# Windowed attention with a routed expert layer on one core: where the second products of nine expert slots are formed by seven products of halves

## The chip, the core and the metric

One Trainium2 chip, one core of it. The program has one launch. The metric is the device time in microseconds (us), the median of three runs; lower is better. Engines: TensorE (PE, with its weight loads PEld), VectorE (DVE), ScalarE (ACT), GpSimd (POOL), SyncE (SP), which issues most transfers.

## The reference

```python
def reference(q, k, v, modality_id, w_gate, modality_bias, w1, w2):
    # q, k, v: (8, 8, 576, 64), float32: batch, heads, positions, head size
    scores = q @ k.T / sqrt(64)                  # per batch and head
    scores = where(0 <= row - column < 64, scores, -1e9)
    x = softmax(scores) @ v                      # -> x: (4608, 512), the 8 heads side by side
    logits = x @ w_gate + modality_bias[modality_id]        # 8 experts
    e = argmax(logits, axis=1); g = softmax(logits)[e]
    out[i] = g[i] * (relu(x[i] @ w1[e]) @ w2[e])            # w1: 8 x 512 x 1024, w2: 8 x 1024 x 512
```

Each of the 4608 tokens goes to one expert. With these inputs the busiest expert has 2289 tokens and the second 1841.

## The kernel before

**Attention.** The sequence is cut into blocks of 64 positions; a step `s` of the main loop handles a pair of blocks with all heads, 36 pairs, and each pair passes through the loop's parts in successive steps (scores in step s, probabilities turned and multiplied with v, then logits and routing up to five steps later), so the loop has 40 steps. Every second step a group of 256 tokens is routed; its rows are written to `xs_scratch` in memory, sorted by expert, by indirect transfers from POOL's queue (`scatter`).

**Slots.** The expert layer works on slots of 256 tokens of one expert, read back from `xs_scratch` by a transfer from SP (`load_slot`, called by `fetch`). To keep float32 accuracy, every operand is split into a high and a low part (ACT rounds the high part, DVE subtracts to get the low one), and each product is formed as hi·hi + hi·lo + lo·hi on PE. A slot has the first products (hidden layer, `first`: 96 matmuls of 128x256) and the second ones. A *plain* slot forms the second products directly (`second`: 48 matmuls of 128x512). A *fast* slot cuts both matrices in halves and uses seven products of sums and differences of halves where eight are usual (`fast_step`, `product`: 84 matmuls of 128x256); `left_of`, `right_of` and `rest_of` build the token side's sums on DVE and ACT, `fast_out` adds the seven results up on DVE. The weight side's sums (the names `b11`, `t1` to `t4` in `factors`) are formed once per expert: four differences on POOL for each quarter of w2, then casts on ACT and subtractions on DVE (`combine`).

**Order.** `slot_pieces` is a generator that gives out one *piece* of a slot's PE work at a time (16 for a plain slot, 15 for a fast one). Steps 12 to 39 beside attention call it four times each (`gap`); the seven slots that this covers are plain. After the last step a loop takes the remaining pieces one after the other. `later` holds the work of other engines that follows a piece. The expert with the most expected tokens is X (index 0), the second Y (index 1); both are chosen at the start from the gate's bias. Small tables worked out on DVE (`plan`, and further behind attention) find each slot's row in `xs_scratch`; `EARLY` lists after which routed group T a slot of X or Y is planned, `LATE` the slots that are planned when all tokens are known: those of X and Y, and of "any" expert (whatever is left). Unfilled places would point at dummy rows.

**Weights.** A piece of weights is 128x512 (16 per expert). `weights(s)` loads one, and splits those that have come; behind attention, the pieces of the "any" experts follow the list `swaps` with their positions. `Whi0`/`Wlo0` hold X. `Whi1`/`Wlo1` hold Y, and later an "any" expert. In before, beside attention run four slots of X and three of Y; behind it one of Y, five fast ones of X, two of Y kept back (`held`), three of any and a half slot for what remains.

**Pads.** Behind the last row of each expert in `xs_scratch`, `pad_rows` copies a block of filler rows (SP's queue): eight copies behind attention, before the loads of late slots.

## Time and profile before

| | |
|---|---|
| median of 3 runs | 642.9 us (642.09 to 645.06) |
| profiled execution, its own time | 640.05 us |
| its span | 638.3 us |
| granted clock, mean | 0.999 |
| start-up and steps 0 to 11 | 0 to 98 us |
| steps 12 to 39, with the first seven slots | 98 to 366.5 us |
| remaining slots | 366.5 to 627 us |
| tail (last outputs) | 627 to 638.3 us |

The page lists busy time by engine, then the span in forty slices, the transfers, the chain of work that ended last, and the costliest groups of instructions. Rows of groups read: line, engine, operation, output from inputs, shape and count, then busy time. Rows of a timeline read: start and length in us, engine, line, operation, and in brackets how long the engine was idle before it and on what it waited. `L415` is the matmul in `second`, `L290` that in `first`, `L374` that in `product`, `L265` the turn of a slot's tokens, `L119` the subtraction in `split_lo`, `L301` the one that gives `hl`, `L1405` to `L1411` the weight side's sums, `L892` the indirect write of routed rows, `L206` the load of a slot's tokens, `L1264` the pads.

### The profile page before, as it was taken

What the parts mean: (1) busy time and instruction counts of PE and PEld (TensorE: products, weight loads), DVE (VectorE), ACT (ScalarE), POOL (GpSimd) and SP (SyncE); (2) the same over time, 40 slices, a digit from 0 to 9 for tenths busy, and PEclk for the clock granted to TensorE, in tenths of its full rate; (3) what the DMA queues carried; (4) which work ended last, traced back from release to release, by engine and by line L of the source; (5) the groups of instructions that cost most, each with busy time, mean ns of one, the idle gap of its engine ahead of it and who ended that gap; (6) DMA issues with size and microseconds to landing.
All of it is one profiled execution on the core that took longest, in us unless ns stands there. A gap on an engine that the chain in (4) does not pass through costs nothing. (4 is left out here: it accounts for less than half of the span.)

```text
span 638.3 us, 17909 instructions
## 1 busy us (share of the span) xinstructions
PE 611.4 (96%) x6689; PEld 558.0 (87%) x6689; DVE 403.5 (63%) x1571; ACT 328.5 (51%) x1005; POOL 154.3 (24%) x337
## 2 busy tenths in 40 slices
PE   6898888999999999999999999999999999999996
PEld 3787777898989889899898988999999989989886
DVE  2978977666776676756654255876746755666611
ACT  3888876656665656455644123533433444554411
POOL 5324432042032213320322255111011011101102
PEclk9999999999999999999999999999999999999999
DMA  9989894774876674552323476021105076777300
GB/s 170 184 194 249 233 222 133 180 167 121 184 177 151 140 177 106 142 137 57 111 75 110 123 205 242 20 67 51 50 34 198 16 223 198 211 243 240 109 1 36
DMA packets 142120, 90.72 MB, mean 142 GB/s; under 512 B 118954, under 2 KB 118992, under 8 KB 141904
## 3 DMA queue, kind: packets, MB, share of 16 engines
q1 hardware_dynamic: 133344, 70.07, 44.8%
q0 software_dynamic: 5856, 18.92, 8.0%
q10 hardware_dynamic: 2832, 0.59, 0.6%
q8 instruction: 53, 0.87, 0.6%
q14 instruction: 35, 0.29, 0.2%
HBM read 70.11 MB, written 23.91 MB: 147 GB/s over the span
## 5 line engine op out<-in xcount | busy, mean ns | idle before, releaser
L290 PE MATMUL em<-xh,Whi 128*128 128x256 f32 x400 | 102.8, 291 | 1.2 <-DVE xl L196 1.0
L290 PE MATMUL em<-xh,Wlo 128*128 128x256 f32 x400 | 98.2, 279 | 0.0
L765 ACT ACTIVATE ss<-ss,mn 128x128 f32<-128x128 f32 x240 | 94.0, 397 | 2.6 <-DVE mn L753 2.6
L429 POOL DMA_INDIRECT out_dram<-y,id x36 | 37.5, 1042 | 219.3 <-DVE y L394 74.4
L415 PE MATMUL y<-Whi,hh 128*128 128x512 f32 x208 | 86.6, 416 | 0.0
L415 PE MATMUL y<-Wlo,hh 128*128 128x512 f32 x208 | 81.6, 392 | 2.2 <-DVE e_take L154 2.2
L415 PE MATMUL y<-Whi,hl 128*128 128x512 f32 x208 | 81.5, 392 | 0.0
L290 PEld LDWEIGHTS em<-xh,Whi 128*128 128x128 f32 x400 | 75.3, 188 | 2.2 <-DVE xl L196 1.6
L290 PEld LDWEIGHTS em<-xh,Wlo 128*128 128x128 f32 x400 | 75.4, 188 | 0.5
L774 ACT COPY pT<-tp 128x512 f32<-128x512 f32 x59 | 32.6, 589 | 78.6 <-PE tp L595 74.3
L753 DVE CUSTOM_DVE_ANT_0 ss<-sp,masks 128x128 f32<-128x128 f32 x240 | 53.5, 287 | 18.4 <-PE sp L736 16.2
L301 DVE SCALAR_TENSOR_TENSOR hl<-em,hh 128x512 fp32r<-128x512 f32 x40 | 27.6, 690 | 57.1 <-ACT hh L300 57.1
L290 PE MATMUL em<-xl,Whi 128*128 128x256 f32 x400 | 63.2, 280 | 0.0
L892 POOL DMA_INDIRECT xs_scratch<-xa,idx x36 | 36.2, 1007 | 81.4 <-DVE lm L835 26.2
L290 PEld LDWEIGHTS em<-xl,Whi 128*128 128x128 f32 x400 | 53.7, 188 | 0.0
L791 PEld LDWEIGHTS av<-ve,pT 128*64 128x64 f32 x576 | 36.3, 138 | 16.4 <-issue 8.4
L300 ACT ACTIVATE hh<-em 128x512 fp32r<-128x512 f32 x40 | 23.6, 591 | 48.1 <-PE em L290 44.1
L791 PE MATMUL av<-ve,pT 128*64 128x64 f32 x576 | 41.0, 225 | 7.2 <-DVE ve L666 3.3
L415 PEld LDWEIGHTS y<-Whi,hl 128*128 128x128 f32 x208 | 39.0, 188 | 8.8
L765 ACT ACTIVATION_READ_ACCUMULATOR ss<-ss,mn 128x1 f32 x240 | 46.4, 193 | 0.0
L415 PEld LDWEIGHTS y<-Wlo,hh 128*128 128x128 f32 x208 | 39.2, 189 | 7.6 <-DVE e_take L154 2.5
L415 PEld LDWEIGHTS y<-Whi,hh 128*128 128x128 f32 x208 | 39.1, 188 | 5.6 <-ACT Whi L112 0.3
(341 smaller groups left out, 1535.3 us busy)
## 6 DMA issues: line engine op xcount, KB each, us to landing
xt<-xs_scratch SPq DMA_DIRECT2D x18, 514.0 KB
y<-in_moe_w_dram SPq DMA_DIRECT2D x32, 256.0 KB
vo<-in_v_dram SPq DMA_DIRECT2D x27, 256.0 KB
vo<-in_moe_w_dram SPq DMA_DIRECT2D x27, 256.0 KB
ss<-in_moe_w_dram SPq DMA_DIRECT2D x27, 256.0 KB
pT<-in_moe_w_dram SPq DMA_DIRECT2D x18, 256.0 KB
xs_scratch<-xs_scratch SPq DMA_DIRECT2D x8, 514.0 KB
qk<-in_q_dram SPq DMA_DIRECT2D x16, 256.0 KB
```

Of the source, the lines that this page charges most:

```text
L290: nc.tensor.matmul(out=hb[:, i * TP:(i + 1) * TP], lhsT=w[buf][:, c0:c0 + P], rhs=x[:, c * TP:(c + 1) * TP], start=(n == 0), stop=(n == le ...
L300: nc.scalar.activation(out=hh, in_=hb, func=AF.Relu),
L301: nc.vector.scalar_tensor_tensor(out=hl, in0=hb, scalar=0.0, in1=hh.bitcast(F32), op0=ALU.max, op1=ALU.subtract)))
L415: nc.tensor.matmul(out=sl["y", t], lhsT=h[:, i * TP + t * P:i * TP + (t + 1) * P], rhs=w[buf][:, c0:c0 + DM], start=(k == 0 and n == 0), s ...
L429: ins = nc.gpsimd.indirect_dma_start(out=out, out_offset=bass.IndirectOffsetOnAxis(ap=sl["id"][:, t:t + 1], axis=0), in_=y, in_offset=None ...
L753: nc.vector.tensor_tensor_reduce(out=ss[a][:, hp, :], in0=sp[a][:, hp * P:(hp + 1) * P], in1=mask, scale=-1.0 / 8.0, scalar=3.0e38, op0=AL ...
L765: nc.scalar.activation(out=ss[a][:, hp, :], in_=ss[a][:, hp, :], func=AF.Exp, bias=mn[:, h:h + 1], scale=-1.0, accum_out=sm[:, h:h + 1])
L774: nc.scalar.copy(out=pT, in_=pp)
L791: nc.tensor.matmul(out=av[c * W64:(c + 1) * W64, 2 * hp + a], lhsT=pT[:, i:i + W64], rhs=(vo if c else ve)[p][:, 2 * hp + a, :], start=Tru ...
L892: ins = nc.gpsimd.indirect_dma_start(out=xs, out_offset=bass.IndirectOffsetOnAxis(ap=idx[:, j:j + 1], axis=0), in_=xg[j], in_offset=None)
```

## The change

- The seven slots beside attention are all X's, and plain (`PLAIN = 7`). Behind attention come two slots of X and seven of Y, all nine fast, then two of any expert and the half slot. `EARLY` has one slot each for T = 2, 4, ..., 16; the doubled plans and `held` go.
- Memory for weights is cut into X's four tiles `M0` to `M3` and the stock `S0`, `S1`, `S2`. X's sums for fast slots lie in `S0`; Y's w1 in `S1`, `S2`. Y's w2 comes late, into `M0`, `M1`, which held X's w1, when the last X slot no longer needs it. The first "any" expert goes to `M2`, `M3` and `S0` during four of Y's slots, one weight piece per four products.
- X's sums are formed in steps 16 to 19 beside attention, Y's in steps 36 to 39 (`SUMS`, `sums_load`, `combine`, `sums_parts`), with one more call of `weights(s)` in step 13; then Y's w1 from step 20 on. Y's w2 itself and the one factor left out follow behind attention (`y_quarters`, `y_fourth`), with three of the four POOL differences made a second time.
- In a fast slot, the next slot's tokens are fetched three products later, and the token side's sums are formed after the first and second product (`sums_of`, `run_after`), the rest after the third and fourth.
- Ten pad copies (X's and Y's first, then the eight experts', those already done sent to spare rows), from a later point on, one each four products.

```diff
-    EARLY = ((2, (0, 1)), (4, (0, 1)), (6, (0, 1)), (8, (0, 1)), (9, (1, 2)), (10, (1, 2)), (11, (1, 2)),
-             (12, (0, 2)), (13, (0, 2)), (15, (0, 2)))
+    EARLY = tuple((T, (0, 1)) for T in (2, 4, 6, 8, 10, 12, 14, 16))
-    LATE = ((0, False), (0, False), (0, True), (1, True), (0, True), (1, True))
-    NPIN = 2
+    LATE = ((0, False),) + ((1, False),) * 7 + ((2, True), (3, True), (2, True))
+    NPIN = 7
-    MIXED = 7
+    PLAIN = 7
...
-    stock = [wpool.tile([P, 2 * WC], F32, name=f"W{part}1") for part in ("hi", "lo")]
-    Whi = [wpool.tile([P, 2 * WC], F32R, name="Whi0"), None]
-    Wlo = [wpool.tile([P, 2 * WC], F32R, name="Wlo0"), None]
+    stock = [wpool.tile([P, 2 * WC], F32, name="S0")] + [wpool.tile([P, WC], F32, name=f"S{n}") for n in (1, 2)]
+    w_x = [wpool.tile([P, WC], F32R, name=f"M{n}") for n in range(4)]
+    store = {0: w_x}
+    def wap(buf, part, c0, n):
+        return store[buf][part + 2 * (c0 // WC)][:, c0 % WC:c0 % WC + n]
...
-        fast = n_slots[0] > MIXED and buf == 0 and whichever is None
+            fast=n_slots[0] > PLAIN and whichever is None)
...
             if i == 1 and sl["fast"]:
                 later.append(lambda: (left_of if k < 2 else right_of)(sl, k % 2, hb))
+                if k >= 2:
+                    after.append(lambda: sums_of(sl, k % 2, hb))
...
             if sl["fast"]:
-                first(sl, 1, 0)
-                yield
-                first(sl, 1, 1)
-                yield
-                first(sl, 2, 0)
-                yield
-                nxt = fetch()
-                first(sl, 2, 1)
-                yield
+                for k in (1, 2):
+                    for i in range(2):
+                        first(sl, k, i)
+                        yield
                 fast_step(sl, "p1")
+                run_after()
                 yield
                 first(sl, 3, 0)
                 yield
+                nxt = fetch()
                 first(sl, 3, 1)
                 yield
                 fast_step(sl, "p7")
-                later.append(lambda: rest_of(sl))
+                run_after()
                 yield
                 fast_step(sl, "p2")
+                run_after()
+                later.append(lambda: rest_of(sl, "s2"))
                 yield
                 fast_step(sl, "p4")
+                later.append(lambda: rest_of(sl, "s4"))
...
-            pieces.extend((x, c) for x in range(2) for c in PIECE_ORDER)
+            pieces.extend((0, c) for c in PIECE_ORDER)
...
+    def combine(x, y, full=True):
+        b11, b12, b21, b22 = x[:, 0:half], x[:, half:DM], y[:, 0:half], y[:, half:DM]
+        for o, a, b in ((b11, b12, b11), (b12, b22, b12), (b22, b22, b11), (b21, b21, b22)):
+            if full or o is not b12:
+                nc.gpsimd.tensor_tensor(out=o, in0=a, in1=b, op=ALU.subtract)
+    def put_parts(src, hi, lo):
+        nc.scalar.copy(out=hi, in_=src)
+        nc.vector.tensor_tensor(out=lo, in0=src, in1=hi.bitcast(F32), op=ALU.subtract)
+    def sums_parts(x, j):
+        a, b = sums_x.pop((x, j))
+        f13, f2 = combos[x][0:2]
+        put_parts(a, f13[0][:, j, :], f13[1][:, j, :])
+        put_parts(b[:, half:DM], f2[0][:, j, :], f2[1][:, j, :])
+        if not x:
+            f4 = combos[x][2]
+            put_parts(b[:, 0:half], f4[0][:, j, :], f4[1][:, j, :])
+    SUMS = {FIRST + 4 + j: (0, j) for j in range(4)}
+    SUMS.update({NPR + j: (1, j) for j in range(4)})
...
     for s in range(NPR + 4):
+        if s == FIRST + 8:
+            store[1] = store[3] = [wpool.tile([P, WC], F32R, name=f"S{n}") for n in (1, 2)] + w_x[0:2]
+            pieces.extend((1, c) for c in (0, 2, 4, 6, 1, 3, 5, 7))
-        n_tick = 6 if s < FIRST else 5
+        n_tick = 6 if s < FIRST or j else 5
...
             high(s)
+        if s in SUMS:
+            combine(*sums_x[SUMS[s]])
...
         if n_gap > 0 and s != FIRST:
+            if s == FIRST + 1:
+                weights(s)
             gap(it, True)
...
             weights(s)
+        if s in SUMS:
+            sums_parts(*SUMS[s])
+        if s + 1 in SUMS:
+            sums_load(*SUMS[s + 1])
...
+    at_ = begin_of[slot_y - 1] + 7
+    pairs_y = [[load(at_, 8 + j + 4 * i, lambda: evs[1]) for i in range(2)] for j in range(4)]
+    for n, i in enumerate((0, 5, 6, 7)):
+        task(at_ + i, y_quarters(n), *pairs_y[n])
+    for n, i in enumerate((8, 10, 13, 14)):
+        task(at_ + i, y_fourth(n), *pairs_y[n])
+    for x, (buf, at_, gap_) in enumerate(((2, begin_of[slot_y + 1], 4), (3, begin_of[slot_a], 1), (2, begin_of[slot_a + 1], 1))):
+        for n, c in enumerate(PIECE_ORDER):
+            task(at_ + n * gap_, whole_piece(buf, c, ("any", x)), load(at_ + n * gap_, c, lambda x=x: any_of(x)))
...
     while next(it, "end") != "end":
...
-        if pads and waited > SLOT_PIECES:
+        if len(pads) > E + 1:
+            if t > begin_of[slot_y - 2]:
+                pad_rows(pads.pop(0))
+        elif len(pads) > E:
+            if not todo or todo[0][2] != 0 or todo[0][1] is not None:
+                pad_rows(pads.pop(0))
+        elif pads and t >= begin_of[slot_y] + 16 and waited % 4 == 0:
             pad_rows(pads.pop(0))
```

The order of instructions on three engines, at the places where other engines wait or are waited for. First DVE in step 14, before: `hl` is the low part of a hidden layer (128x512), `Wlo0` the low part of X's weights, the rows `L836` to `L848` belong to the routing.

```order
L301 SCALAR_TENSOR_TENSOR hl_2285<-em_2223,hh_2284 128x512 [waits Activation_49]
L836 TENSOR_TENSOR lg_1977<-lg_1977,lm_2167 128x16
L840 SCALAR_TENSOR_TENSOR wn_2169<-lg_1977,desc_194 128x16 [waits DVE_49]
L842 TENSOR_REDUCE wm_2170<-wn_2169 128x2 [waits DVE_49]
L843 TENSOR_TENSOR oh_1803<-wn_2169,wm_2170 128x16 [waits DVE_49]
L848 TENSOR_REDUCE oh_2171<-oh_1803 128x8 [waits DVE_49]
L119 TENSOR_TENSOR Wlo0_67<-y_2101,Whi0_66 128x512 [waits DMAHW6_49]
```

After, the same stretch (`M3` is the low part of X's second matrix, `M2` its high part):

```order
L848 TENSOR_TENSOR lg_1980<-lg_1980,lm_2179 128x16 [waits DVE_49]
L117 TENSOR_TENSOR M3_70<-y_2062,M2_69 128x512 [waits DMAHW6_49,Activation_49]
L153 TENSOR_TENSOR e_n_p_2093<-sel2_71,cnt_2091 1x8
L158 TENSOR_REDUCE e_n_2094<-e_n_p_2093 1x1 [waits DVE_49]
L147 SCALAR_TENSOR_TENSOR e_at_2095<-e_n_2094,room2_229,row2_72 1x1 [waits DVE_49]
L141 TENSOR_SCALAR rows_0_4_2096<-e_at_2095 1x1 [waits DVE_49]
L714 COPY kT_101<-tp_2294 128x2x2x128 [waits PE_49]
L304 SCALAR_TENSOR_TENSOR hl_2293<-em_2235,hh_2292 128x512 [waits Activation_49]
```

The piece of weights whose low part stood behind `hl` and the routing's rows now stands ahead of them.

Next POOL around the last routed group, before: `gate` and `id` come from a slot's tokens, `xa` are the rows that are written to `xs_scratch`.

```order
L274 COPY gate_6640<-xt_6529 128x2 [waits DMAHW1_49]
L276 CAST id_6642<-xt_6529 128x2 [waits DMASW3_49,DMASW0_49]
L891 COPY xa4_105<-idc_202 128x1 [waits DMASW7_49]
L892 DMA xs_scratch<-xa4_105,idx_6605 39168x514 [waits DVE_49,Pool_49]
L891 COPY xa0_101<-idc_202 128x1 [waits DMASW1_49]
L892 DMA xs_scratch<-xa0_101,idx_6605 39168x514 [waits Pool_49]
```

After:

```order
L1176 TENSOR_TENSOR vo_6588<-vo_6588 128x256 [waits DMAHW0_49,PE_49]
L1176 TENSOR_TENSOR vo_6588<-ss_6589,vo_6588 128x256 [waits DMAHW1_49,Pool_49]
L1176 TENSOR_TENSOR ss_6589<-ss_6589,vo_6588 128x256 [waits Activation_49,Pool_49]
L1176 TENSOR_TENSOR ss_6589<-ss_6589 128x256 [waits Pool_49]
L903 COPY xa4_108<-idc_205 128x1 [waits DMASW7_49]
L904 DMA xs_scratch<-xa4_108,idx_6642 39680x514 [waits DVE_49,Pool_49]
L903 COPY xa0_104<-idc_205 128x1 [waits DMASW0_49]
L904 DMA xs_scratch<-xa0_104,idx_6642 39680x514 [waits Pool_49]
```

The four differences of Y's last quarter stand ahead of the last two writes of routed rows.

Last SP at the end of attention, before: `vo` and `ss` take pieces of w2 for the sums, `masks` is the room for tables.

```order
L204 TENSOR_LOAD rows_2_12_5154
L206 DMA xt_6803<-xs_scratch 128x2x514 [waits DMAHW0_49,DMAHW1_49,PE_49,Pool_49]
L105 DMA vo_6860<-in_moe_w2_dram 128x512
L105 DMA ss_6862<-in_moe_w2_dram 128x512 [waits DMAHW2_49]
L1263 TENSOR_LOAD masks_143 [waits DVE_49,Pool_49]
L1264 DMA xs_scratch<-xs_scratch 16x8224 [waits DMAHW3_49,DMAHW0_49]
```

After:

```order
L201 TENSOR_LOAD rows_0_16_6463 [waits DVE_49]
L203 DMA xt_6551<-xs_scratch 128x2x514 [waits DMASW5_49,DMASW4_49,DMAHW7_49,DMASW1_49,DMASW0_49]
L108 DMA vo_6588<-in_moe_w2_dram 128x512 [waits DMAHW0_49,PE_49]
L108 DMA ss_6589<-in_moe_w2_dram 128x512 [waits DMAHW2_49,DVE_49,Pool_49]
L1357 TENSOR_LOAD masks_146 [waits DVE_49,Pool_49]
L1358 DMA xs_scratch<-xs_scratch 16x8224 [waits DMAHW7_49]
L201 TENSOR_LOAD masks_146 [waits DVE_49,Pool_49]
L203 DMA xt_6892<-xs_scratch 128x2x514 [waits DMASW7_49,DMAHW2_49,DMASW6_49,DMAHW3_49,PE_49,Pool_49]
```

The load of slot 7's tokens now stands ahead of the last loads for the sums, and waits for the writes of the group that planned it; the first pad copy stands ahead of the next slot's load.

More of the change, by code (lines that the diff above doesn't have):

```diff
@@ L198, in ready @@
     def ready(sl, c0):
-        c = c0 // WCH
-        assert (sl["buf"], c) not in pieces + [r[1:] for r in raws + halves]
-        assert sl["any"] is None or (sl["any"], c) not in [w[2:] for w in swaps]
+        assert (sl["key"], c0 // WCH) in have
     def load_slot(row_ap, late, nb):
@@ L219, in tile_window_attn_moe @@
     later = []
+    after = []
+    mixed = []
     scattered = []
     n_slots = [0]
-    n_early = [0]
-    held = []
     factors = {}
@@ L234, in bank, with run_after @@
         return ps_t.tile([P, 512], F32, name="tp")
+    def run_after():
+        later.extend(after)
+        after.clear()
     def run_later():
@@ L243, in fetch @@
         row, late, buf, whichever, need = todo.pop(0)
-        assert late is not None or not pads
+        assert late is not None or len(pads) <= {0: E + 1, 1: E}.get(buf, 0)
         assert late is None or late in scattered
@@ L248, in fetch @@
         n_slots[0] += 1
-        fast = n_slots[0] > MIXED and buf == 0 and whichever is None
-        return dict(xt=load_slot(row, late, nb), buf=buf, any=whichever, nb=nb, fast=fast)
+        return dict(
+            xt=load_slot(row, late, nb), buf=buf, nb=nb, key=buf if whichever is None else ("any", whichever),
+            fast=n_slots[0] > PLAIN and whichever is None)
     def slot_pieces():
@@ L285, in first @@
             hi, lo = sl["x"]
-            mm = [(w, c, hi) for c in range(NC1) for w in (Whi, Wlo)] + [(Whi, c, lo) for c in range(NC1)]
+            mm = [(w, c, hi) for c in range(NC1) for w in (0, 1)] + [(0, c, lo) for c in range(NC1)]
             for n, (w, c, x) in enumerate(mm):
@@ L410, in second @@
             hi, lo = sl["h", k]
-            mm = [(h, w, i) for i in range(2) for h, w in ((hi, Whi), (hi, Wlo), (lo, Whi))]
+            mm = [(h, w, i) for i in range(2) for h, w in ((hi, 0), (hi, 1), (lo, 0))]
             for n, (h, w, i) in enumerate(mm):
@@ L439, in half_first @@
             hi, lo = sl["x"]
-            mm = [(x, w, c) for c in range(NC1) for x, w in ((hi, Whi), (hi, Wlo), (lo, Whi))]
+            mm = [(x, w, c) for c in range(NC1) for x, w in ((hi, 0), (hi, 1), (lo, 0))]
             for m, (x, w, c) in enumerate(mm):
@@ L464, in half_second @@
             yp = ps_m.tile([P, DM], F32, name=f"y{a}")
[L465 removed]
+            mm = [(w, n, c, lo) for n in range(2) for c in range(HP) for w, lo in ((0, 0), (1, 0), (0, 1))]
             for m, (w, n, c, lo) in enumerate(mm):
@@ L939, in plan @@
         stt(pl, nm, take, float(TP), room, ALU.mult, ALU.add, out=room)
-        for i, x in reversed(list(enumerate(range(xs_.start, xs_.stop)))):
-            (held if x and n_early[0] > MIXED else todo).append((rows[0:1, i:i + 1], f"scatter_after_{T}", x, None, need))
-            n_early[0] += 1
+        for i, x in enumerate(range(xs_.start, xs_.stop)):
+            todo.append((rows[0:1, i:i + 1], f"scatter_after_{T}", x, None, need))
     def choose():
@@ L1366, in tile_window_attn_moe @@
             n_of[buf] += 1
-            continue
-        last_use[buf] = len(early) + n_any - 1
     last.append(True)
-    ahead = []
+    tick(ready_p - issued[0], table=True)
     waited = 0
-    t13 = [att.tile([P, 2, HP, GBLK, W64], F32R, name=nm).rearrange("p g h j i -> p (g h j i)") for nm in ("kT", "qT")]
-    t2 = [work.tile([P, 2, H, D], F32R, name="qk", bufs=2).rearrange("p t h d -> p (t h d)") for _ in range(2)]
-    half = DM // 2
-    inner = [x[0][:, WC:2 * WC].rearrange("p (c n) -> p c n", n=DM) for x in (Whi, Wlo)]
@@ new lines, in tile_window_attn_moe, with load, task @@
+    slot_y = len(EARLY) + 1
+    slot_a = slot_y + 7
+    w2 = [x.rearrange("p (c n) -> p c n", n=DM) for x in w_x[0:2]]
+    make_factors(1, *combos[1], w2, half)
+    store[2] = [w_x[2], w_x[3], sums_home[:, 0:WC], sums_home[:, WC:2 * WC]]
+    loads = []
+    tasks = []
+    raw_of = {}
+    def load(pos, c, ev):
+        loads.append([pos, c, ev, None])
+        return len(loads) - 1
+    def task(pos, f, *ids):
+        for i in ids:
+            loads[i][3] = len(tasks)
+        tasks.append((pos, f, ids))
@@ L1440, in tile_window_attn_moe @@
+        while n_load < len(loads) and loads[n_load][0] <= t + RAWS and (
+                n_load < RAWS or loads[n_load - RAWS][3] < n_task):
+            _, c, ev, _ = loads[n_load]
+            raw_of[n_load] = load_piece(raw_tile(), ev(), c)
+            n_load += 1
+        if n_task < len(tasks) and tasks[n_task][0] <= t:
+            _, f, ids = tasks[n_task]
+            f(*(raw_of[i] for i in ids))
+            n_task += 1
+    assert n_task == len(tasks) and not todo and not pads
     manual.__exit__(None, None, None)
```

227 lines of the change are left out of this document (115 added, 112 removed).

## The prediction

> **What bounds the kernel now.** I read the page first (busy shares, slices, chain), then busy time by stage, then windows of single slots, and last the places where TensorE (PE) idles.
>
> ```profile
> PE 611.4 (96%) x6689; PEld 558.0 (87%) x6689; DVE 403.5 (63%) x1571; ACT 328.5 (51%) x1005; POOL 154.3 (24%) x337
> ...
> PEclk9999999999999999999999999999999999999999
> ...
> PE 48%; DVE 1%; ACT 0%; issue 0%; POOL 0%; POOLq 0%; ACTq 0%
> ```
>
> PE is busy 96% of the span at an undisturbed clock; on the chain, no other engine holds more than 1%. The stages (start-up, steps beside attention, slots behind it, tail):
>
> ```profile
> 0.00:98.00 98.00, 80.33 (x1384) 69.58 (x1385) 72.36 (x401) 74.53 (x283) 37.62 (x108) 1.00 0.94 204
> 98.00:366.50 268.50, 264.58 (x3344) 237.51 (x3341) 171.69 (x815) 148.71 (x515) 67.18 (x136) 1.00 0.54 136
> 366.50:627.00 260.50, 260.36 (x1916) 244.93 (x1915) 157.00 (x351) 104.70 (x207) 46.06 (x88) 1.00 0.41 130
> ```
>
> After the stretch and its length come busy PE, weight load, DVE, ACT and POOL, then clock and DMA share. Behind attention PE idles 0.14 us of 260.5, beside it 3.92 of 268.5. So time comes from fewer PE microseconds, or from those few idle ones; and any engine that makes PE wait adds directly.
>
> **The change part by part.** *The products.* Four more slots use seven products of halves: nine where there were five. The twelve groups of 48 second products, 128x512, lose four, so 192 matmuls go, and 4 x 84 = 336 of 128x256 come. The first products stay. What a slot of each kind takes, in before, from the first product of one to that of the next (four fast slots, then two plain ones):
>
> ```profile
> 394.75:416.94 22.19, 22.05 (x184) 21.59 (x182) 17.01 (x60) 9.49 (x21) 5.75 (x10) 1.00 0.21 71
> 416.94:438.97 22.03, 22.03 (x188) 22.03 (x189) 16.03 (x52) 8.41 (x18) 2.44 (x6) 1.00 0.24 63
> 438.97:460.90 21.93, 21.93 (x191) 21.93 (x189) 13.46 (x31) 8.41 (x18) 2.45 (x6) 1.00 0.15 51
> 460.90:482.82 21.92, 21.92 (x190) 21.92 (x189) 13.44 (x31) 8.41 (x18) 2.46 (x6) 1.00 0.15 48
> ...
> 550.79:573.78 22.99, 22.99 (x154) 20.87 (x153) 15.16 (x26) 12.05 (x23) 2.93 (x6) 1.00 0.73 222
> 573.78:596.79 23.01, 23.01 (x154) 20.87 (x152) 15.17 (x26) 12.05 (x23) 2.76 (x6) 1.00 0.70 216
> ```
>
> A plain slot is 23.00, an uncrowded fast one 21.93: 1.07 less, for four slots **-4.3**. The same from single matmuls:
>
> ```profile
> 367.42 0.39 PE L415 MATMUL y<-Whi,hh 128*128 128x512 f32 x1
> 367.65 0.39 PE L415 MATMUL y<-Wlo,hh 128*128 128x512 f32 x1
> ...
> 372.00 0.28 PE L290 MATMUL em<-xh,Whi 128*128 128x256 f32 x1
> 372.11 0.28 PE L290 MATMUL em<-xh,Wlo 128*128 128x256 f32 x1
> 372.23 0.28 PE L290 MATMUL em<-xh,Whi 128*128 128x256 f32 x1
> ```
>
> From start to start, 0.23 for 512 columns and 0.115 for 256: 336 x 0.115 - 192 x 0.23 = -5.5; the two decimals make this coarse (0.12 for 0.115 gives -3.8). I take the windows and keep -3.8 to -4.5. The Trainium skill speaks against this step: "TensorE: Matmul & The Clock Gate", section "Back-to-back issue gap", gives sustained spacings of about 81 ns at 128 columns and 131 ns at 512. An estimate of mine between them, 98 ns at 256, would make the four slots 336 x 98 - 192 x 131 ns = +7.8 us. The windows above contradict it for this kernel.
>
> *Crowding of fast slots.* The first fast slot of before (DVE 17.01 of 22.19) was 0.26 over the uncrowded one, the second (16.03) 0.10, together 0.36. In after, the first three fast slots carry the planner's small operations, twelve POOL differences and the splits of Y's second matrix; four later ones take one piece of a remaining expert each four products (4 x 0.68 of DVE on 13.46 is 16.2, as in the row that cost 0.10). 3 x 0.26 + 4 x 0.10 - 0.36 = **+0.8**. Ends: -0.36 (none is crowded) and 9 x 0.26 - 0.36 = +2.0; I stay with the rows of like DVE load.
>
> *The one long stall.* PE's largest wait beside attention stands in step 14:
>
> ```profile
> 109.55 0.50 PE L415 MATMUL y<-Whi,hh 128*128 128x512 f32 x1
> 112.29 0.50 PE L415 MATMUL y<-Wlo,hh 128*128 128x512 f32 x1 [2.24 <-DVE e_take L154]
> ...
> 106.72 0.68 DVE L119 TENSOR_TENSOR Wlo<-y,Whi 128x512 fp32r<-128x512 f32 x1
> ...
> 110.03 0.69 DVE L301 SCALAR_TENSOR_TENSOR hl<-em,hh 128x512 fp32r<-128x512 f32 x1 [0.29 <-ACT hh L300]
> ...
> 111.55 0.68 DVE L119 TENSOR_TENSOR Wlo<-y,Whi 128x512 fp32r<-128x512 f32 x1
> ```
>
> The product with the low part waits for the split at 111.55, which ends 112.23; e_take, named as releaser, is only the next on DVE. After makes an extra round of weight pieces in step 13, so this split moves ahead of the hl at 110.03, into the place of the one at 106.72. That is over 2 us before the need: **-2.2** (between 0, if the next piece is late in its turn, and -2.24). That next piece is wanted a group of second products later.
>
> *More weight pieces beside attention* (40, not 32; behind it 56, not 72) *and the sums of both second matrices there*. For one set of four quarters before needs, in the first slot behind attention, where nothing waited:
>
> ```profile
> L1405 POOL TENSOR_TENSOR vo<-vo x3: 741/753/783, 378.6 to 397.0; 128x256 f32<-128x256 f32 x3
> L1405 POOL TENSOR_TENSOR ss<-pT,ss x1: 1878/1878/1878, 386.4 to 386.4; 128x256 f32<-128x256 f32 x1
> ...
> L1406 ACT CAST kT<-vo x2: 621/621/621, 380.3 to 398.6; 128x512 fp32r<-128x512 f32 x2
> ...
> L1407 DVE TENSOR_TENSOR qT<-vo,kT x2: 693/694/694, 380.9 to 399.3; 128x512 fp32r<-128x512 f32 x2
> ...
> L1410 ACT CAST qk<-ss x2: 401/404/407, 381.1 to 401.2; 128x256 fp32r<-128x256 f32 x2
> ...
> L1411 DVE TENSOR_TENSOR qk<-ss,qk x2: 406/416/425, 382.1 to 401.9; 128x256 fp32r<-128x256 f32 x2
> ```
>
> Each of eight steps (16 to 19, 36 to 39) gets four POOL differences, 4 x 0.75 = 3.0 (4.7 if one or two are drawn out like the 1.88), and casts of 0.62 + 2 x 0.40 on ACT, subtractions of 0.69 + 2 x 0.41 = 1.5 on DVE. An even and an odd step of before:
>
> ```profile
> 170.82:181.26 10.44, 10.44 (x140) 9.43 (x137) 6.77 (x31) 6.45 (x23) 3.50 (x6) 1.00 0.48 99
> 181.26:192.27 11.01, 10.88 (x145) 9.61 (x141) 8.60 (x36) 6.36 (x22) 2.88 (x6) 1.00 0.85 207
> ```
>
> With them DVE comes to 8.3 of 10.44 (10.1 of 11.01 in an odd step), ACT to 7.9, POOL to 6.5. I cost both moves at nothing; the cover is that PE works from queues filled a step ahead. If it is gone, a step lasts as long as load, differences and casts together (rival C). The early plans of routing fall from ten to eight, two fewer small rows of DVE: nothing.
>
> *The end of attention.* Here the last sums of Y, the last scatter and slot 7's tokens come together.
>
> ```profile
> DMA to landing us min/median/max: 3.1/3.7/8.8
> ...
> 359.18 0.99 POOL L892 DMA_INDIRECT xs_scratch<-xa,idx  x1 [6.60 <-DVE lm L835]
> ...
> 372.65 0.98 POOL L892 DMA_INDIRECT xs_scratch<-xa,idx  x1 [10.58 <-DVE idx L904]
> ...
> 368.16 0.54 PE L265 MATMUL em<-ident_r,xt 128*128 128x128 f32 x4
> ...
> 371.75 0.28 PE L290 MATMUL em<-xh,Whi 128*128 128x256 f32 x1
> ```
>
> In after, slot 7's tokens wait for the plan's scatter of step 16's group, whose first half begins at 359.18 in before, the second 1.5 later. With 3.7 to land (the first row, of the scatters) and as much for the load they are there about 365.5 to 368, against a need at 368.16. Four differences then precede the last scatter on POOL (372.65 here, idle 10.58 before it), and two casts, 0.62 + 0.40 on ACT, stand ahead of the copies of slot 7's tokens. I take half of that 1.02, **+0.5**; ends 0 and +3.4 (1.02 and a load late by one 2.4 us copy).
>
> *Copies of pads, queue SP.* Ten, not eight, and moved behind the loads:
>
> ```profile
> 374.60 9.11 SPq L1264 DMA_DIRECT2D xs_scratch<-xs_scratch  x7
> 393.58 0.41 SPq L206 DMA_DIRECT2D xt<-xs_scratch  x1
> ...
> SPq L206 <- DMA xs_scratch<-xs_scratch: 7.3, 1, 7.3
> ```
>
> Seven in a row held SP's next token load for 7.3 us, 2.5 each, and PE didn't notice. After lets only two ahead of the loads it needs, and one each four products later: nothing, hidden by a fetch that still runs half a slot (11 us) ahead of its use. Fetching three products later in a fast slot (3/15 of 21.93 = 4.4) takes from that lead, and leaves about 7 against 3.7 + 2.5.
>
> **The sum.** -4.3 - 2.2 + 0.8 + 0.5 = **-5.2**. The profiled execution took 640.05 (span 638.3 and 1.75 around it), which is 2.85 under the median, 642.9; 640.05 - 5.2 = 634.85, on the scale of the median **637.7**. Own range, from the terms' ends: 636 to 641.
>
> **The rivals.** *B, the chain at the end of attention is late.* Y's last sums reach PE as factors only from the tenth slot on, so it's the scatter and slot 7's tokens that count. Against it: half a step of slack by the rows above; for it: the PE queue has nothing else there. Price +2.4 to +5, with -5.2: 640 to 643; the middle, 641.5.
>
> *C, slower: POOL's differences hold DVE.* Rows of before, side by side:
>
> ```profile
> 388.37 0.15 DVE L154 TENSOR_TENSOR masks<-used,masks 1x2 f32<-1x2 f32 x1
> ...
> 381.53 0.69 DVE L154 TENSOR_TENSOR masks<-masks,used 1x2 f32<-1x2 f32 x1
> ```
>
> The same tiny operation takes 0.15 alone and 0.69 during a difference. The Trainium skill has a rule for it, in "SBUF — State Buffer", section "SBUF: two separate sides": VectorE's second port pair is shared with GpSimd as an exclusive lock, and the loser waits for the whole instruction. Its direction agrees with these two rows. As a mechanism here: 4 x 0.54 is 2.2 of DVE time per step, and 32 differences stand beside attention where none stood. It decides where a step's chain of load 3.7, differences up to 4.7 and casts and subtractions 3.0 (11.4) is longer than the step (10.44): +1.0 in each of 8 steps, +8, and a DVE that comes to 10.5 of 10.44 drags ACT in order: to +12. 637.7 + 8 to 12 = 646 to 650. Against it: DVE's spare 3.7 us, and PE's idle of 0.00 in the even step.
>
> *D, more gain.* No slot is crowded, and the end costs nothing: -4.3 - 2.2 - 0.4 = -6.9, and 1 of the other 1.7 us of idle beside attention goes: 635 to 636.
>
> *E, the change doesn't do it:* fewer slots are filled than there are fast places. With 7 plain and 9 fast places for two experts that hold at least nine and seven full slots in these inputs, all are filled: no chance.
>
> *F, 256 columns cost more than half of 512* (what the Trainium skill's spacings say, told above). At 0.23 for 512 the break-even is 192 x 0.23 / 336 = 0.131. At 0.13, a hundredth over the largest spacing in the rows, the products bring -0.5 instead of -4.3, and the time is 641.5. The windows speak against it.
>
> **How the numbers follow.** Chances: forecast 0.59, B 0.22, C 0.08, D 0.10, F 0.01. The range reaches from D's lower end to B's upper, **634.8 to 643**. About 0.5% (3.2 us) is what a measurement of this kernel can tell: faster is below 639.7, that is the forecast but for its upper tail (0.54 of 0.59), D, and little of B (0.02): 0.66; same 0.26 (the tail, B and F); slower 0.08.
>
> **What would show it.** Fast slots of 22.0 to 22.2 from the eighth on to the sixteenth; no PE wait over 1 us at step 14; PE idle behind attention still under 1 us; steps 16 to 19 as long as before. A wait before slot 7's first product would show B; PE waits in those eight steps ended by ACT or DVE, C. The forecast is wrong if PE's busy time doesn't fall by about 4 us.

## The result, and the profile after

The changed kernel took 646.76 us (median of 13 runs, 645.46 to 648.42) against 642.09 of the kernel before on the same chip (13 runs, 640.83 to 645.06): ratio 1.0069, 95% interval 1.0056 to 1.0082. It is 4.7 us slower, where 5.2 us faster was forecast. The profiled execution took 646.22 (span 644.5).

The page of the changed kernel, busy shares, clock by slices and chain:

```profile
PE 616.2 (96%) x6830; PEld 567.4 (88%) x6831; DVE 429.4 (67%) x1645; ACT 339.8 (53%) x1049; POOL 176.6 (27%) x365
...
PEclk9999989999999999999999999999999999999999
...
PE 82%; DVE 7%; DMA 4%; SPq 4%; issue 2%; ACT 1%; POOL 0%; POOLq 0%; DVEq 0%; ACTq 0%
```

PE's busy time should have fallen by 4 us; it rose by 4.8 (611.4 to 616.2). The slots behind attention are near the forecast: the second, the third and the ninth fast one, then the plain one that follows the nine (columns as in the prediction).

```profile
402.41:424.58 22.17, 22.09 (x190) 21.88 (x188) 15.34 (x47) 10.24 (x24) 5.21 (x9) 1.00 0.17 56
424.58:447.54 22.96, 22.27 (x189) 22.04 (x189) 22.26 (x68) 10.68 (x25) 12.74 (x15) 1.00 0.25 80
...
557.34:579.29 21.95, 21.95 (x190) 21.95 (x189) 13.54 (x31) 8.20 (x18) 2.44 (x6) 1.00 0.36 134
579.29:602.34 23.05, 23.05 (x161) 21.19 (x160) 13.20 (x23) 10.42 (x20) 2.65 (x6) 1.00 0.57 182
```

The third fast slot is the one with the twelve POOL differences. The time was lost beside attention, in the even steps. One of them, step 28, before and after, as windows from its first score matmul to that of the next step:

```profile
258.01:268.46 10.45, 10.45 (x140) 9.44 (x137) 6.69 (x36) 5.94 (x22) 3.51 (x6) 1.00 0.42 107
```

```profile
262.42:274.37 11.95, 11.50 (x140) 9.88 (x136) 6.94 (x32) 5.95 (x22) 3.84 (x11) 1.00 0.39 116
```

The same 140 matmuls take 1.5 us longer. PE's list of waits in the changed kernel has a row that the kernel before lacks, its score matmuls waiting for "issue", that is, for nothing that the profile shows:

```profile
PE sp L748 <- issue: 2.7, 10, 0.3
```

The timeline of that step's start (`sp<-kT,qT` are its 32 score matmuls, `xs_scratch<-xa,idx` the two indirect writes of a routed group):

```profile
261.67 1.05 POOL L904 DMA_INDIRECT xs_scratch<-xa,idx  x1 [12.88 <-DVE xl L195]
...
262.42 1.84 PE L748 MATMUL sp<-kT,qT 64*64 64x128 f32 x28
...
263.00 0.47 PEld L748 LDWEIGHTS sp<-kT,qT 64*64 64x64 f32 x12 [0.17 <-issue]
...
263.21 0.99 POOL L904 DMA_INDIRECT xs_scratch<-xa,idx  x1 [0.28 <-issue]
263.81 0.21 PEld L748 LDWEIGHTS sp<-kT,qT 64*64 64x64 f32 x4 [0.33 <-issue]
...
264.56 0.46 PE L748 MATMUL sp<-kT,qT 64*64 64x128 f32 x4 [0.30 <-issue]
```

In the kernel before the same 32 are one run without a break:

```profile
258.01 1.10 PE L736 MATMUL sp<-kT,qT 64*64 64x128 f32 x32
```

From the start of a step's first score matmul to that of its last are 0.84 us in the kernel before. In the changed one they are 1.2 to 2.7 in the eleven even steps 14 to 34. Added up over those steps, the time above 0.84 is 11.4 us; below it is called **the gaps** (an expectation below has 11.3 and 9.3 for what is 11.4 and 9.4 here). Their sum is larger than the loss. And one thing stands there that did not before: the writes. At two places of a step, `tick(n_tick)` gives out the next of the routing's small operations, five at a time before, now six in odd steps (`n_tick = 6 if s < FIRST or j else 5`). The last six of a group end with the one that issues its two writes. With the sixth, the writes move from 4 to 8 us behind an even step's first score matmul to 0.4 to 1.5 us ahead of it (the first write) and 0 to 1.2 behind (the second).

### The profile page after: what moved, and what is told of

It reads as the page before. It is cut to its first block, busy times and chain, and to the rows that moved or that the text cites. A ratio compares the mean times of both kernels' runs of the same rounds, so it can differ in the third digit from the quotient of the medians.

```text
span 644.5 us, 18326 instructions
## 1 busy us (share of the span) xinstructions
PE 616.2 (96%) x6830; PEld 567.4 (88%) x6831; DVE 429.4 (67%) x1645; ACT 339.8 (53%) x1049; POOL 176.6 (27%) x365
## 4 chain that ended last, share of the span: by engine, by line
PE 82%; DVE 7%; DMA 4%; SPq 4%; issue 2%; ACT 1%; POOL 0%; POOLq 0%; DVEq 0%; ACTq 0%
PE em L291 21%; PE y L428 16%; PE tp L608 9%; PE sp L291 9%; PE y L387 6%; PE sp L748 6%; PE av L803 5%; PE sp L387 3%; SPq L700 3%; PE tp L828 2%; DMA S<-in_k_dram 2%; PE av L387 2%; DMA xs_scratch<-xa,idx 1%; PE y L482 1%; DMA qk<-in_k_dram 1%
## 5 line engine op out<-in xcount | busy, mean ns | idle before, releaser
L428 PE MATMUL y<-M,hh 128*128 128x512 f32 x256 | 83.6, 408 | 0.0
L291 PE MATMUL em<-xh,M 128*128 128x256 f32 x544 | 80.2, 290 | 1.1 <-DVE xl L195 1.0
L291 PEld LDWEIGHTS em<-xh,M 128*128 128x128 f32 x544 | 69.4, 191 | 1.8 <-DVE xl L195 1.3
L748 PE MATMUL sp<-kT,qT 64*64 64x128 f32 x1152 | 49.1, 282 | 5.9 <-issue 2.7
L428 PE MATMUL y<-M,hl 128*128 128x512 f32 x128 | 50.3, 393 | 0.0
L428 PEld LDWEIGHTS y<-M,hh 128*128 128x128 f32 x256 | 43.8, 188 | 6.0
L291 PE MATMUL em<-xl,M 128*128 128x256 f32 x272 | 43.4, 282 | 0.0
L291 PEld LDWEIGHTS em<-xl,M 128*128 128x128 f32 x272 | 37.0, 190 | 0.0
L291 PE MATMUL em<-xh,S 128*128 128x256 f32 x256 | 35.4, 280 | 0.8 <-DVE xl L195 0.7
L291 PE MATMUL sp<-xh,S 128*128 128x256 f32 x256 | 35.2, 280 | 0.0
```

The lines of the kernel that those rows point to most:

```text
L291: nc.tensor.matmul(out=hb[:, i * TP:(i + 1) * TP], lhsT=wap(buf, w, c0, P), rhs=x[:, c * TP:(c + 1) * TP], start=(n == 0), stop=(n == len( ...
L428: nc.tensor.matmul(out=sl["y", t], lhsT=h[:, i * TP + t * P:i * TP + (t + 1) * P], rhs=wap(buf, w, c0, DM), start=(k == 0 and n == 0), sto ...
L748: nc.tensor.matmul(out=sp[a][c * W64:(c + 1) * W64, hp * P:(hp + 1) * P], lhsT=qT[rows, g // GBLK, hp, g % GBLK + c], rhs=blocks(hp, g, g ...
```

## The experiments

In the expectations, theory 1 says that writes ahead of score matmuls make the gaps; the others are told in each. Each session ran on one chip, with the kernel before beside it.

**First session.** The changed kernel with five operations (`a1`), with six but the writes held back (`a3`), and the kernel before with six (`b1`) or with extra small writes at the place in question (`m1`).

```diff
  a1, b1: the number of routing operations
-        n_tick = 6 if s < FIRST or j else 5        # a1: back to before
+        n_tick = 6 if s < FIRST else 5
-        n_tick = 6 if s < FIRST else 5             # b1: as after
+        n_tick = 6 if s < FIRST or j else 5
  a3: the writes go to a list, emptied in the next even step
+            if step_now[0] > FIRST:
+                go_later.append(go)
...
         tick(2)
+        while j == 0 and go_later:
+            go_later.pop(0)()
  m1: two more writes of 8 bytes a row, at the end of odd steps
         tick(n_tick)
+        if j == 1 and FIRST < s < NPR:
+            extra(s)
```

> The changed kernel with one number undone: five instead of six routing operations at the two places of an odd step, as in the kernel before, so that the two writes of routed rows (POOL) are issued in the middle of an even step and not at its very start. Theory 1 (these writes, issued 0.4 to 1.5 us ahead of an even step's 32 score matmuls, starve TensorE, which then shows gaps called issue): the score groups of steps 16 to 34 last 0.84 us again instead of 1.5 to 2.7, the even steps go from 11.4 back to 10.5, and the time falls by 9 to 11 us, to 635 to 638. Theory 2 (the work moved beside attention, sums and weight pieces, slows the steps): no change, 646 to 647.

> The changed kernel, six operations kept, where only the two POOL writes of routed rows are issued later, behind the second block of small operations of the even step; all of VectorE's routing rows stay where the change has them. Theory 1 (the writes): 635 to 638, score groups 0.84. Theory 3 (the shifted rows of VectorE, or the routing as a whole, hold the scores): 646 to 647, score groups as long as in the changed kernel.

> The kernel before with only that number of the change: six routing operations in odd steps. Nothing else of the change is in it. Theory 1: even steps 16 to 34 get longer by about 1 us each, and the time goes from 642 to 650 to 653. Theory 2: no change, 641 to 643.

> The kernel before plus two extra indirect writes from POOL at the end of each odd step from 13 to 35, 128 rows of 8 bytes each to a scratch of their own (2 KB of data where a real one has 263 KB); the real writes stay where they were. If making and issuing the 128 row transfers is what starves TensorE (theory 1a): score groups of even steps 1.2 to 2.7 us, time 649 to 653. If it is the bytes moved (theory 1b): score groups 0.84, time 642 to 644.

| | median, us | ratio to before (639.9 us) | gaps, us |
|---|---|---|---|
| a1 | 636.1 | 0.9926 (0.9907 to 0.9946) | 0 |
| a3 | 634.6 | 0.9902 (0.9878 to 0.9926) | 0 |
| b1 | 638.1 | 0.9972 (0.9955 to 0.9989) | 0 |
| m1 | 647.1 | 1.0100 (1.0065 to 1.0135) | 0 |

Taken alone, the first two rows look like a proof of theory 1. The other two deny it: `b1` and `m1` have writes ahead of their scores and no gap. `m1` (two runs) has the undisturbed score groups of 1b, but is 7 us longer than the kernel before, in steps 14 and 27 and behind step 35.

**Second session: is it the chip?** Both kernels unaltered; also the stall alone (`b2`, one line added to the kernel before), and six operations only in the last steps (`a4`).

```diff
  b2
         if n_gap > 0 and s != FIRST:
+            if s == FIRST + 1:
+                weights(s)
             gap(it, True)
  a4
-        n_tick = 6 if s < FIRST or j else 5
+        n_tick = 6 if s < FIRST or j and s > 32 else 5
```

> The changed kernel once more, unaltered, beside kernels that differ from it in one number and do not show its gaps before the scores (the first four runs: with the six operations put into the kernel before, the writes of routed rows fall on the same places, and there is no gap; theory 1 is wrong as it was stated). Theory 4 (the gaps belong to this very program, by its exact instruction stream and memory, and come back in every execution): score groups of even steps 1.2 to 2.7 us, 643 to 647. Theory 5 (the gaps came from the state of the chip or the load in which the first executions were made, not from the program): score groups 0.84 and 633 to 637.

> The kernel before, unaltered, for a profile beside that of the others. Theory 4 and 5: score groups 0.84 in all steps; 639 to 643, with the wait of 2.24 us in step 14.

> The kernel before with one part of the change alone: the additional round of weight pieces in step 13. If the prediction's step on the stall holds, step 14 takes 10.5 to 11 us instead of 13.1, and the time falls by 2 to 2.3 us against the kernel before. If the next piece is late in its turn: no change.

> The changed kernel with five routing operations in odd steps up to step 32 and six after it. With five throughout, the stretch between the seventh and the eighth slot's first products took 28.8 us, with six 26.5. If the last group's writes are what the end waits for (rival B): 26.5 here and 633 to 634.5. If it is something else that six operations bring earlier in the steps before: 28.8 and 636.

| | median, us | ratio to before (642.85 us) | gaps, us |
|---|---|---|---|
| changed kernel | 645.0 | 1.0036 (1.0020 to 1.0052) | 9.4 |
| kernel before | 642.4 | 0.9994 | 0 |
| b2 | 639.1 | 0.9952 (0.9933 to 0.9971) | 0 |
| a4 | 636.7 | 0.9916 (0.9893 to 0.9938) | 0.35 |

The gaps are back with the changed kernel. In `a4` only step 34 has one (1.19 instead of 0.84), the only step with writes near its scores. `a4`'s time is over the 633 to 634.5 expected, but slot 6 takes the 26.5 that was. `b2` settles the stall: step 14, in the first profile of before and in `b2`,

```profile
103.18:116.29 13.11, 10.87 (x140) 9.36 (x137) 8.29 (x41) 7.61 (x25) 3.09 (x5) 1.00 0.63 175
```

```profile
104.19:114.66 10.47, 10.47 (x140) 9.43 (x136) 8.03 (x41) 7.41 (x25) 3.09 (x5) 1.00 0.57 148
```

is 2.64 shorter, against 2.2 forecast. Beside `b2`, in the second profile of before, it took 14.53, which makes it 4.06, and the whole of `b2` is 3.1 us faster by its ratio, where 2 to 2.3 were expected: the stall is not of one size, but it goes.

**Third session: is it where instructions lie?** The changed kernel with six tiny POOL instructions (`p1`) or one warm-up matmul (`p3`) more at the start, so that everything behind them is shifted in its stream.

```diff
+    for _ in range(6):
+        nc.gpsimd.memset(pause, 0.0)               # p1
-    WARM = 4, 3
+    WARM = 5, 3                                    # p3
```

> The changed kernel plus six one-element memsets on POOL at its start; nothing in the steps is touched. The gaps come back in every execution of the changed kernel (9.3 and 11.3 us in two profiles), but the kernel before with its writes at the same places has none, nor have steps 22, 26, 30 and 34 of the kernel with later writes. Theory 6 (a property of the exact program, such as where its instruction streams lie, decides whether a write near the scores stalls TensorE): the gaps are gone or of another size, 633 to 642. Theory 7 (something in the steps themselves, the same with or without the memsets): 9 to 11 us of gaps, 643 to 647.

> The changed kernel plus one matmul more among those that keep TensorE busy at the start (two instructions more in its stream). Theory 6, if it is TensorE's own stream: the gaps are gone or of another size, 633 to 642. Theory 7: 9 to 11 us of gaps, 643 to 647.

`p1` took 644.8 (ratio 1.0017, 1.0000 to 1.0033), `p3` 645.4 (1.0031, 1.0008 to 1.0053), with gaps of 9.5 and 9.1 us in the same steps. A shift by a few instructions changes nothing.

**Fourth session.** The changed kernel again, `b1` and `a3` again, and six operations for s > 34 alone (`a5`, the line of `a4` with 34).

> The changed kernel, unaltered, on the same chip as the next two. So far every profile with writes of routed rows close ahead of the scores that had gaps (three chips) and every one that had none (one other chip) came from different chips. Theory 1 with the chip as a second condition (1c): on a chip that shows the gaps here, the next two kernels show them as well, and on a chip that shows none, none of the three does. Theory 8 (a difference between the kernels): gaps of 9 to 11 us here, none in the next two. Time 643 to 647 with the gaps, 634 to 637 without.

> The kernel before with six routing operations, again, beside the changed kernel. Theory 1c: gaps of 7 to 11 us over steps 16 to 34 if the changed kernel has them on this chip, time 648 to 653; none if it has none, 638 to 641. Theory 8: none in either case, 638 to 641.

> The changed kernel with later writes, again; its writes still fall close ahead of the scores in steps 14, 22, 26, 30 and 34. Theory 1c: if the changed kernel has gaps on this chip, gaps of 0.3 to 1.9 us in those steps and in no other, 3 to 5 us in all, 637 to 640. Theory 8: none, 634 to 636.

> The changed kernel with five routing operations in odd steps up to 34, and six in the last ones, so that no write of routed rows stands ahead of any scores and the last group still comes early. Theory 1 and 1c: no gaps on any chip, 6 to 8 us below the kernel before (633 to 636). Theory 8: the same, unless the difference lies elsewhere in the steps.

The unaltered changed kernel took **632.0** us here, ratio 0.9860 (0.9838 to 0.9882) to 640.4 of the kernel before: 8.4 us faster, with no gap in any step. `b1` took 638.8 (0.9980, 0.9962 to 0.9999), `a3` 635.2 (0.9913), `a5` 632.5 (0.9874). So one program is 1.4% faster or 0.4 to 0.7% slower by session. Steps 22 and 18 here, against 12.37 and 11.37 of the first profile:

```profile
145.71:156.19 10.48, 10.48 (x141) 9.45 (x137) 8.66 (x40) 7.08 (x25) 6.23 (x11) 1.00 0.53 160
188.55:199.04 10.49, 10.49 (x141) 9.44 (x137) 7.20 (x38) 6.46 (x23) 3.43 (x8) 1.00 0.63 174
```

What tells the sessions apart is seen in every kernel, in step 6, which lies ahead of the steps that the change touches. It lasts 5.51 or 5.52 us in all eight profiles of the first and fourth session, and 5.97 to 6.03 in all twelve others, both kernels before and after among them. The kernel before in its first profile, and `b1` in the fourth session:

```profile
44.48:50.49 6.01, 4.95 (x106) 4.54 (x102) 4.33 (x25) 5.80 (x24) 4.38 (x7) 1.00 1.16 284
```

```profile
46.38:51.89 5.51, 5.02 (x104) 4.47 (x100) 4.68 (x25) 5.51 (x23) 4.48 (x7) 1.00 1.14 284
```

Steps 8 and 12 go with it (before: 6.03 and 10.96; `b1` in the fourth session: 5.61 and 9.71), and with them the kernel before itself: 642.1 to 643.3 us in five sessions, 639.9 and 640.4 in the two without gaps. Below, a session is *with gaps* if step 6 takes 6.0.

**Fifth session, with gaps.** Open was whether writes ahead of the scores are enough, and whether moving them alone helps.

> The kernel before with six routing operations in the odd steps and nothing else; the same program stood at 638.1 and 638.8 us against 639.9 and 640.4 of the kernel before on two chips on which even the changed kernel shows no gaps among its score matmuls. What is new is the chip. Theory 1c (gaps need two things: the POOL writes issued within some 1.5 us ahead of an even step's score matmuls, and a chip that answers to it): if the kernel before stands near 642 to 643 us on this chip, the score groups of the even steps 14 to 34 take 1.2 us and more instead of 0.84, in sum 8 to 11 us, and the kernel takes 647 to 652 us. Rival 8 (it takes something else of the changed kernel, its products or its weights beside attention, for the gaps to come): on such a chip the score groups stay at 0.84 and the time is 639 to 642 us, a little under the kernel before. If the kernel before stands near 640 us, the chip has no gaps and both theories expect 638 to 639 us: the question then stays open.

> The changed kernel with its six routing operations kept, in which only the POOL writes of an odd step's last routing operation wait until two operations of the next even step are issued; it stood at 634.6 and 635.2 us on two chips without gaps. Theory 1c: on a chip that has gaps (the kernel before near 642 to 643 us) the score groups stay at 0.84 us all the same, since no write is issued ahead of them, and the time is 635 to 638 us, 1% under the kernel before. Rival 8 (the writes' place matters only together with the rest, or not at all): the score groups take 8 to 11 us more in sum and the time is 643 to 648 us. On a chip without gaps both expect 634 to 636 us.

`b1` took 653.2 us (ratio 1.0174, 1.0126 to 1.0221), gaps 12.2 us, a little more than theory 1c expected; `a3` 642.4 (0.9987, 0.9965 to 1.0008), gaps 4.9. `b1` is the kernel before but for the one line. Its step 22 in the fourth session, then in the fifth:

```profile
190.55 1.07 POOL L892 DMA_INDIRECT xs_scratch<-xa,idx  x1 [7.03 <-DVE rs L797]
...
191.24 1.10 PE L736 MATMUL sp<-kT,qT 64*64 64x128 f32 x32
...
192.11 0.96 POOL L892 DMA_INDIRECT xs_scratch<-xa,idx  x1 [0.28 <-DMA qk<-in_q_dram]
```

```profile
195.74 1.07 POOL L892 DMA_INDIRECT xs_scratch<-xa,idx  x1 [7.05 <-DVE rs L797]
...
196.42 0.65 PE L736 MATMUL sp<-kT,qT 64*64 64x128 f32 x13
...
197.28 0.45 PE L736 MATMUL sp<-kT,qT 64*64 64x128 f32 x3 [0.21 <-issue]
197.29 0.96 POOL L892 DMA_INDIRECT xs_scratch<-xa,idx  x1 [0.28 <-DMA qk<-in_q_dram]
...
198.03 0.46 PE L736 MATMUL sp<-kT,qT 64*64 64x128 f32 x4 [0.30 <-issue]
```

The first write begins 0.7 ahead of the scores in both, the second 0.87 behind, and they last as long. Only the scores differ. `a3` fits neither expectation, and for a reason that decides the question: in time, its edit moved only some writes. In steps 14, 22, 26, 30 and 34 they still begin 0.4 to 1.2 us ahead of the scores, and there the score groups take 1.17, 2.64, 1.66, 1.64 and 1.96; in 16, 18, 20, 24, 28 and 32 they don't, and these take 0.83 or 0.84. Step 20, without a write, and step 22, with one, in this one execution:

```profile
168.79 1.10 PE L750 MATMUL sp<-kT,qT 64*64 64x128 f32 x32
```

```profile
189.19 1.07 POOL L906 DMA_INDIRECT xs_scratch<-xa,idx  x1 [1.41 <-DVE rs L811]
...
189.89 0.66 PE L750 MATMUL sp<-kT,qT 64*64 64x128 f32 x14
...
190.79 0.47 PE L750 MATMUL sp<-kT,qT 64*64 64x128 f32 x4 [0.24 <-issue]
```

In a session with gaps, then, these writes are enough and needed. The chip here bears the same number as that of the first session, which had no gaps; if the number means the same chip, it is a condition that comes and goes.

**Sixth session, with gaps.** Is it the data, or the issue of the write? And what does the changed kernel bring with no write ahead of the scores?

> The kernel before with two more POOL indirect writes at the end of each odd step 13 to 35, of 8 bytes a row instead of 2 KB, issued 0.7 to 1.9 us ahead of the next score matmuls and again 0.6 us around their start; everything else, the true writes too, stays where it stood. What matters is whether this chip is in a state that shows gaps (the kernel before near 642 to 643 us and its steps 6 and 8 at 6.0 us; near 640 us and 5.5 to 5.6 us where it shows none). Theory D (the issue of an indirect write is enough, whatever it moves): where gaps are shown, the score groups of the steps 14 to 34 take 1.2 us and more, in sum 8 to 14 us, and the kernel takes 652 to 662 us. Theory M (it takes the 256 KB that a true write moves): the score groups stay at 0.84 us, in sum under 1 us, and the kernel takes 643 to 650 us, as the extra work alone cost 7 us where no gaps were. Where none are shown: 647 us, and the question stays open.

> The changed kernel with six routing operations only in the odd step 35, so that no POOL write is issued ahead of a score matmul of a later step; it took 632.5 us where no gaps were shown. Theory 1c (writes ahead of the scores, in a state that answers to them, are the whole loss): where gaps are shown the score groups stay at 0.84 us in sum within 0.5 us, and the time is 633 to 637 us, 1.0 to 1.4% under the kernel before, since the start, which is slower there by 1 to 2 us, is not touched. Rival 8 (part of the loss comes from something else of the changed kernel): 638 to 645 us with score groups over 0.84 us. Where no gaps are shown both expect 632 to 633 us.

`m1` took 658.2 us (ratio 1.0222, 1.0155 to 1.0289), 9.1 us of it gaps, with writes of 8 bytes a row. Its step 22:

```profile
197.78 1.05 POOL L1153 DMA_INDIRECT xm_scratch<-idc,mx  x1 [7.26 <-DVE Wlo L119]
...
198.52 1.03 PE L736 MATMUL sp<-kT,qT 64*64 64x128 f32 x16
...
199.79 0.45 PE L736 MATMUL sp<-kT,qT 64*64 64x128 f32 x5 [0.24 <-issue]
...
200.52 0.65 PE L736 MATMUL sp<-kT,qT 64*64 64x128 f32 x11 [0.28 <-issue]
```

So the volume isn't the cause. Nor do the write's packets have to be under way. In the first profile of the changed kernel, step 22's scores run from 193.79 and make their first pause from 194.18 to 194.64, right behind the end of the first write on POOL (193.10 and 1.07 long). From 193.80 to 194.64 the view of the transfers has one queue alone, which isn't POOL's:

```profile
q1 hardware_dynamic: 734, 0.18, 96.1%
```

POOL's queue (`q0`) moved its first packet of the step at 195.1, and the two queues that the page calls instruction (`q8`, `q14`) moved none from 193.1 to 196.5, so this pause was no wait for instructions to land either. What is left is POOL's issuing of the write.

`a5` took 636.4 (ratio 0.9897, 0.9861 to 0.9932) with no gap, and the score group of step 22 whole again:

```profile
192.94 1.10 PE L748 MATMUL sp<-kT,qT 64*64 64x128 f32 x32
```

It is 6.4 us under the kernel before in a session with gaps (`a4` stood at 6.2), and within 0.5 us of the changed kernel where there are none.

## Why the prediction was wrong

The step that failed is one that the prediction doesn't have: the sixth routing operation in odd steps, a line of the diff that is no term of its sum. Where it says of the moved weights and sums "I cost both moves at nothing; the cover is that PE works from queues filled a step ahead", the writes that a further operation brings forward are not among what was moved, though they are transfers from POOL's queue and were moved past the next step's scores. The gaps that they made come to 11.4 us in the first comparison. The order of instructions on POOL would have shown it: in every group behind step 12 the two writes stand ahead of the even step's `rs<-sm`, where before they stand behind it.

No row of the first profile gives that price: in no step behind 12 does a write there stand near the scores, and that steps 6, 8 and 12 (first write 0.6 to 0.7 us behind the first score matmul) were 0.4 to 1.3 us longer than without gaps is seen only beside the other sessions. Whether their writes did that isn't shown: their score groups take 0.83. But the place could have been named, as a term with an open loss, and the range would have been wider.

The terms, each by its windows (us):

| term | forecast | measured |
|---|---|---|
| four more fast slots | -4.3 | -4.2: 21.95 for 23.00 |
| crowding | +0.8 | +1.0, the remainder: slots 7 to 16 are 3.2 less together |
| stall in step 14 | -2.2 | -2.6 (`b2` against the first profile) |
| sums and weights beside attention | 0 | +0.4: steps 16 to 19 43.38 for 42.95 of `b1` (fourth session) |
| end of attention | +0.5 | 0: slot 6 26.50 and 26.51 |
| tail | 0 | +0.7: 42.17 for 41.47 |
| sixth operation, without gaps | none | -1.6 to -1.8 (`b1`) |
| gaps | none | +11.4 |

They add up to -6.4 without gaps and to +5.0 with them; the medians of the first comparison have +4.7, which is closer than the terms are known. Without gaps the changed kernel measured -8.4, so there, too, the -5.2 of the forecast would have been 3.2 us short. Of the 2.0 us between -6.4 and -8.4, 0.8 lie in steps 20 to 34 (158.49, against 159.29 in `b1` of that session). The rest isn't located, as the kernel before has no profile from such a session.

*The sum's own bounds.* The range "from the terms' ends: 636 to 641" is narrower than these ends: the upper ones (-3.8, 0, +2.0, +3.4) come to +1.6, which is 644.5. The measured loss lies beyond that as well. E counts nine full slots of X; 2289 tokens are eight and 241 more, which changes no term.

*Products and F.* The price of 256 columns was right, and F is out.

*Crowding* came in one piece: the slot with twelve differences has DVE busy 22.26 of 22.96, and PE waited 0.69 for it.

*B* named a true place, and its own rows left less slack than it says: 359.18 and twice 3.7 is 366.6, not 365.5, and the second half comes at 368.1, against a need at 368.16. With five operations (`a1`) slot 6 takes 28.77 instead of 26.50, PE busy for 26.75 of it:

```profile
341.54:370.31 28.77, 26.75 (x232) 23.35 (x230) 15.75 (x58) 8.44 (x18) 16.98 (x26) 1.00 0.37 124
```

```profile
354.00:380.50 26.50, 26.50 (x231) 23.56 (x229) 15.68 (x58) 8.53 (x18) 15.96 (x24) 1.00 0.34 117
```

The 2.3 us are about B's lower price (2.4); 1.36 of them are PE's wait right ahead of slot 7's first product, the sign that the prediction names for B. The sixth operation, needed only in the odd steps from 35 on (`a5`: 26.59 and 26.53), takes the wait away, and holding its writes back (`a3`, first session: 28.54) brings it again; I hadn't connected the two.

*C* had its price wrong, but its mechanism is there. In the changed kernel without gaps, step 18, with four differences, took 10.48 (first row of the fourth session), before 10.46. But with five operations (`a1`, `a4`, `a5`) steps 16 to 19 took 44.85 against 43.22 before: steps 17, 18 and 19 are 0.4 to 0.7 longer, and in each PE waits 0.4 to 0.5 for DVE, where before it waited 0.1 in step 17 alone. At the end of step 17 in `a5`, DVE's three subtractions (`L1180`) run beside POOL's differences (`L1176`) and take 2.71; PE's wait follows in step 18:

```profile
141.17 3.58 POOL L1176 TENSOR_TENSOR S<-S 128x256 f32<-128x256 f32 x4
...
142.33 2.71 DVE L1180 TENSOR_TENSOR S<-S,S 128x512 fp32r<-128x512 f32 x3
...
146.15 0.52 PE L608 MATMUL tp<-ident_r,ss 128*128 128x128 f32 x3 [0.49 <-DVE lg L833]
```

In the changed kernel of the same session six operations put the differences elsewhere. POOL is idle for 3.85 until it issues a write at 145.02, and the same three subtractions take 1.35:

```profile
144.13 1.35 DVE L1180 TENSOR_TENSOR S<-S,S 128x512 fp32r<-128x512 f32 x3
...
145.02 1.08 POOL L904 DMA_INDIRECT xs_scratch<-xa,idx  x1 [3.85 <-DVE S L1180]
```

This agrees with the exclusive lock of the Trainium skill ("SBUF — State Buffer", section "SBUF: two separate sides"). It doesn't explain all of the 1.6 us: ahead of step 17's wait the subtractions took their 1.35. And 1.6 in four steps is far from the 8 that C reckons with in eight.

*D* would have come nearest where there were no gaps, but not by its reasons: one slot was crowded by 1.0, and the end cost nothing only through the sixth operation.

## What to carry to other kernels

A change to how many small operations a step gives out moves transfers, too: list every transfer that ends up ahead of a dense run of short matmuls, and price it as a range with a loss in it. Run the unaltered change beside each experiment in the same session; `a1` and `a3` alone would have "proved" the right cause on a chip where it wasn't acting. And take an extra operation only where it pays: the odd steps from 35 on gave the 2.3 us at the end of attention, the earlier ones the loss where there were gaps, and 1.5 us in steps 16 to 19 (43.38 for 44.85) where there were none.

## What the hardware showed

Indirect writes that POOL began in the last 1.5 us or so ahead of a run of 32 short matmuls (0.84 us, 27 ns apart) broke that run up with pauses of up to 0.6 us, 0.2 to 1.9 us a step, in five sessions of seven, and never in the other two; 8 bytes a row did it (9.1 us of gaps) as 2 KB did (9.1 to 12.2). Nothing of it shows in the clock (1.00 in those steps). Step 6 told in all twenty profiles which kind of session it was (5.5 or 6.0 us).

Why the pauses come is open. The Trainium skill ("DMA: Bandwidth & Descriptors", section "SWDGE vs HWDGE vs iDMA") says that GpSimd writes the descriptors of such a transfer into rings in SBUF. That would fit a cost which doesn't depend on the bytes; no run here shows it to be the cause, and neither it nor any run says why sessions differ.

Three DVE subtractions took 2.71 us beside POOL's differences, and 1.35 without them (`a5` and the changed kernel, fourth session).
